# Attention and MoE in one kernel: the start written out by hand, with the first two batches alternating over d_ff

## The chip, the cores and the metric

The kernel runs on one core of a Trainium2 chip. The metric is the device time of one execution in microseconds (us), as the median of several runs. A profiled execution of the same program gives the trace that the following parts read.

## What is computed

The reference first runs a two-stage attention for 8 batches and 8 heads (sequence 576, head size 64, 32 packed queries `p`), and then a feed-forward layer on the 4608 x 512 result, with d_ff = 2048.

```python
def _attn_ref(q, k, v, p):
    scale = 1.0 / np.sqrt(q.shape[-1])
    def sm_attn(qq, kk, vv):
        s = scale * np.matmul(qq, kk.transpose(0, 1, 3, 2))
        s = s - np.max(s, axis=-1, keepdims=True)
        a = np.exp(s)
        a = a / (np.sum(a, axis=-1, keepdims=True) + 1e-09)
        return np.matmul(a, vv)
    p_packed = sm_attn(p, k, v)
    return sm_attn(q, p_packed, p_packed)

def _moe_ref(x, w_in, w_out):
    h = x @ w_in
    sp = np.where(h > 20.0, h, np.log1p(np.exp(np.minimum(h, 20.0))))
    return (h * np.tanh(sp)) @ w_out
```

The two weights arrive as float64 words, which the kernel converts itself.

## The kernel before

**The work of one batch.** Attention of a batch has two halves of four heads (`g`). Keys are turned on TensorE (PE) and copied out of PSUM (L118, L106), scores are taken, their largest value subtracted, and the exponential taken in one instruction for both halves (`score`, `exps`). Queries, the attention weights and the packed values follow (`turn`, `turn_weights`, `values`, `turn_values`); `match` takes the second scores and `weigh` their softmax, and leaves it as a high and a low part, `aT_hi` and `aT_lo`. The packed values never go into an output of attention: `packed_w` (L331) multiplies them into a chunk of four d_ff blocks of w_in (`ps_w`, L338), so that the first layer of the feed-forward part is one product of `wp_hi`, `wp_lo` with `aT_hi`, `aT_lo`.

**The main loop** (L501) has one step `t` for each block of 128 columns of d_ff of each batch: 16 steps a batch, 128 in all, and two more at the end. A step has the first product (`up`, two column halves, twelve matmuls, L388), Mish on ScalarE (ACT, L391 and L393), the split of the result `g` into `g_hi` (a cast) and `g_lo` on VectorE (DVE, L400 and L401, `halves`), and the second product (`down`, four row chunks of three matmuls, L405 to L407) of the block two steps earlier (`LAG`). Four accumulators of PSUM collect a batch's 16 blocks and are copied out after the last (`evac`). The last 64 columns of two batches are multiplied together, four blocks at a time (`split`, `down_rest`). Every fourth step ends with the `packed_w` of the next chunk. The attention of batch b+1 is a generator, of which up to three pieces are taken in each step of batch b; whatever is left is done before the batch's first `packed_w` (`together(gen)`).

**The weights.** There are 16 tiles of w_in (four chunks of four, `load_wi`) and 16 of w_out (`load_wo`). Each is loaded as pairs of 32-bit words into one of three staging buffers (`staged`, L304) and converted by two Copy instructions of ACT (L295, L296) and four operations of DVE (L297 to L302); w_out is then split into a high and a low part (L312, L313). Converted w_in goes to DRAM as well, from where later batches fetch it. Four tiles are converted during batch 0's attention, five ahead of the loop, and then two in each step, so all 32 are done by step 11.

**Order.** Only PE runs in the order in which the program is written (L474). The order of DVE, ACT and of the DMA queue (SP, from which every load and store is issued) comes from the planner, which fits each instruction in where its engine is free in a simulated run. Keys, queries and values share seven buffers of two heads each (`KVB`); a batch has twelve such tiles.

## Time and profile before

| | |
|---|---|
| median of three runs | 821.02 us (820.76 to 822.58) |
| the profiled execution's own time | 822.64 us |
| its span in the trace | 820.9 us |
| PE busy | 768.2 us (94%) |
| weight loads of PE | 610.4 us (74%) |
| DVE busy | 420.6 us (51%) |
| ACT busy | 336.0 us (41%) |
| moved by DMA | 90.02 MB, 110 GB/s over the span |

The span runs from the first instruction to the last. Times in the trace count from its start. A matmul's busy time is pipelined: the distance from one start to the next says how fast PE runs, and the granted clock (1 is full speed) whether it was throttled. In the strip of 40 slices a slice is 20.5 us and a digit is the busy share in tenths.

### The profile page before, as it was taken

The numbers are of one execution on the slowest core, as the hardware profiler recorded it, in microseconds if no ns is written. First come the engines' busy times: TensorE is split into PE (matmuls) and PEld (weight loads), VectorE is DVE, ScalarE is ACT, GpSimd is POOL, SyncE is SP. The second block draws the span as 40 slices with busy tenths as digits, with TensorE's granted clock in tenths as the row PEclk, the third lists the DMA queues.
The fourth block names the chain that finished last, engine by engine and source line by source line (L and its number), as shares of the span: only waits on it lengthen the run. The fifth ranks groups of instructions, "written<-read, shape, count | busy, mean of one in ns | idle before, by whom it ended". The sixth has DMA issues, their size and how long they took to land.

```text
span 820.9 us, 13745 instructions
## 1 busy us (share of the span) xinstructions
PE 768.2 (94%) x5584; PEld 610.4 (74%) x5584; DVE 420.6 (51%) x812; ACT 336.0 (41%) x766; POOL 0.7 (0%) x6
## 2 busy tenths in 40 slices
PE   6607789999999999999999999999999999999997
PEld 4406667787788787877778787877778787888886
DVE  4799895744373435544373435544373445533332
ACT  3557583435242353235242353335242353332221
POOL 0000000000000000000000000000000000000000
PEclk6557789999999999999999999999999999999999
DMA  9967673144311533144411433144311421131002
GB/s 256 287 226 231 207 243 95 52 139 138 110 52 52 143 95 111 52 138 139 110 52 52 132 107 111 52 137 140 110 52 52 122 67 53 52 103 52 1 1 64
DMA packets 43966, 90.02 MB, mean 110 GB/s; under 512 B 8576, under 2 KB 27008, under 8 KB 43904
## 3 DMA queue, kind: packets, MB, share of 16 engines
q1 hardware_dynamic: 43904, 89.15, 35.8%
q8 instruction: 44, 0.72, 0.4%
q14 instruction: 18, 0.15, 0.1%
HBM read 75.50 MB, written 13.63 MB: 109 GB/s over the span
## 4 chain that ended last, share of the span: by engine, by line
PE 88%; DMA 5%; DVE 4%; issue 1%; ACT 1%; SPq 0%; ACTq 0%
PE ps_h L388 25%; PE acc L405 16%; PE acc L407 14%; PE acc L406 14%; PE ps_kq L118 4%; DMA w_st<-in_moe_w_in_dram 4%; PE ps_w L338 4%; PE ps_s L127 3%; PE ps_rest L405 2%; PE ps_rest L407 2%; PE ps_rest L406 2%; PE ps_pp L209 1%; PE ps_a L200 1%; DMA k_t<-in_k_dram 1%; DMA w_st<-in_moe_w_out_dram 1%
## 5 line engine op out<-in xcount | busy, mean ns | idle before, releaser
L405 PE MATMUL acc<-wo_hi,g_hi 128*128 128x512 f32 x512 | 216.5, 423 | 0.0
L391 ACT ACTIVATE g<-ps_h 128x288 f32<-128x288 f32 (+1 forms) x256 | 98.5, 385 | 286.5 <-PE ps_h L388 250.5
L407 PE MATMUL acc<-wo_hi,g_lo 128*128 128x512 f32 x512 | 203.4, 397 | 0.0
L406 PE MATMUL acc<-wo_lo,g_hi 128*128 128x512 f32 x512 | 203.3, 397 | 0.0
L388 PE MATMUL ps_h<-aT_hi,wp_hi 128*128 128x288 f32 x512 | 159.3, 311 | 21.8 <-ACT aT_hi L263 21.1
L400 DVE CAST g_hi<-g 128x512 fp32r<-128x512 f32 x128 | 54.5, 426 | 239.7 <-ACT g L391 239.7
L388 PE MATMUL ps_h<-aT_lo,wp_hi 128*128 128x288 f32 x512 | 153.2, 299 | 1.9 <-DVE aT_lo L264 1.9
L388 PE MATMUL ps_h<-aT_hi,wp_lo 128*128 128x288 f32 x512 | 153.3, 299 | 0.0
L405 PEld LDWEIGHTS acc<-wo_hi,g_hi 128*128 128x128 f32 x512 | 97.4, 190 | 42.7 <-issue 20.4
L388 PEld LDWEIGHTS ps_h<-aT_hi,wp_hi 128*128 128x128 f32 x512 | 98.1, 192 | 39.6 <-ACT aT_hi L263 23.2
L407 PEld LDWEIGHTS acc<-wo_hi,g_lo 128*128 128x128 f32 x512 | 96.9, 189 | 23.7 <-DVE g_lo L401 0.2
L388 PEld LDWEIGHTS ps_h<-aT_lo,wp_hi 128*128 128x128 f32 x512 | 98.4, 192 | 11.3 <-DVE aT_lo L264 2.5
L406 PEld LDWEIGHTS acc<-wo_lo,g_hi 128*128 128x128 f32 x512 | 97.6, 191 | 8.6
L388 PEld LDWEIGHTS ps_h<-aT_hi,wp_lo 128*128 128x128 f32 x512 | 98.4, 192 | 0.0
L401 DVE TENSOR_TENSOR g_lo<-g,g_hi 128x512 fp32r<-128x512 f32 x128 | 88.2, 689 | 5.9
L350 DVE TENSOR_TENSOR wp_lo<-ps_w,wp_hi 128x512 fp32r<-128x512 f32 x64 | 41.3, 682 | 19.0 <-ACT wp_hi L349 19.0
L349 ACT CAST wp_hi<-ps_w 128x512 fp32r<-128x512 f32 x64 | 34.3, 588 | 32.8 <-PE ps_w L338 32.8
L338 PE MATMUL ps_w<-wi,ppT 64*32 64x512 f32 x512 | 35.7, 615 | 0.0
L118 PE MATMUL ps_kq<-ident,k_t 96*128 96x96 f32 x192 | 27.0, 273 | 9.0 <-issue 4.9
L118 PEld LDWEIGHTS ps_kq<-ident,k_t 96*128 96x128 f32 x192 | 23.1, 158 | 16.4 <-issue 6.4
L118 PE MATMUL ps_kq<-ident,q_t 96*128 96x96 f32 x192 | 26.6, 267 | 6.5 <-issue 2.9
L118 PEld LDWEIGHTS ps_kq<-ident,q_t 96*128 96x128 f32 x192 | 22.6, 154 | 13.1 <-issue 4.6
(81 smaller groups left out, 727.0 us busy)
## 6 DMA issues: line engine op xcount, KB each, us to landing
wi<-w_in_f SPq DMA_DIRECT2D x56, 512.0 KB, 4.5
k_t<-in_k_dram SPq DMA_DIRECT2D x32, 288.0 KB, 3.6
q_t<-in_q_dram SPq DMA_DIRECT2D x32, 288.0 KB, 4.8
v_t<-in_v_dram SPq DMA_DIRECT2D x32, 288.0 KB, 3.6
w_st<-in_moe_w_in_dram SPq DMA_DIRECT2D x16, 512.0 KB, 5.2
w_st<-in_moe_w_out_dram SPq DMA_DIRECT2D x16, 512.0 KB, 4.3
out_dram<-o SPq DMA_DIRECT2D x24, 192.0 KB, 2.5
w_in_f<-wi SPq DMA_DIRECT2D x8, 512.0 KB, 5.0
```

What stands on the lines that cost most here:

```text
L118: nc.tensor.transpose(out=ps[:, h, :], in_=of_slot(src, g, h)[:, i, :], identity=ident[:R, :R])
L127: nc.tensor.matmul(out=ps[u][h * NP:(h + 1) * NP, :], lhsT=packT[u * D:(u + 1) * D, h * NP:(h + 1) * NP], rhs=xT[u * D:(u + 1) * D, :, h, ...
L338: nc.tensor.matmul(out=ps[g][h * NP:(h + 1) * NP, :], lhsT=ppTb[row:row + D, g, h * NP:(h + 1) * NP], rhs=wis[b, c, g][row:row + D, h // 2 ...
L349: nc.scalar.copy(out=hi, in_=ps[g])
L350: nc.vector.tensor_tensor(out=lo, in0=ps[g], in1=hi.bitcast(F32), op=ALU.subtract)
L388: nc.tensor.matmul(out=ps, lhsT=w[:, fs], rhs=a[:, g, cs], start=(n == 0), stop=(n == 5))
L391: nc.scalar.activation(out=self.act[:, hf * HALF:hf * HALF + m], in_=ps[:, :m], func=AF.Mish)
L400: nc.vector.tensor_copy(out=hi, in_=self.act)
L401: nc.vector.tensor_tensor(out=lo, in0=self.act, in1=hi.bitcast(F32), op=ALU.subtract)
L405: nc.tensor.matmul(out=acc, lhsT=hi[:, cs], rhs=wh, start=start, stop=False)
L406: nc.tensor.matmul(out=acc, lhsT=hi[:, cs], rhs=wl, start=False, stop=False)
L407: nc.tensor.matmul(out=acc, lhsT=lo[:, cs], rhs=wh, start=False, stop=stop)
```

## The change

The change rewrites the start of the program. The parts are these:

- Ahead of the loop and in steps 0 to 9 (`START`), DVE, ACT and SP also run in the order in which the program is written. From step 10 on they are planned as before; PE is written throughout.
- The blocks run in another order: batch 0's blocks 0 to 7, batch 1's 0 to 15, batch 0's 8 to 15, then batches 2 to 7 as before (`TURNS`, `order`). Batch 0's accumulators are copied out as parts after its first turn, and added to the second turn's. A pair's rest product comes when the later of its two chunks is done (`paired`).
- A weight is an object with `fetch` (its load), `words` (the two Copies), `join` (the four operations of DVE) and `done` (the store, or the split of w_out). Of the first 16 weights, 14 are loaded into eight more buffers (tag `late`), which w_out's tiles 8 to 15 take over later; the others use two staging buffers. `conversion` fetches several weights ahead in the start and two ahead later. Two weights are converted in steps 0 and 1 and one in each later step.
- Batch 1's attention is taken in steps 0 to 5, up to five pieces a step. Batch 2's begins at step 20. Batches 2 and 3 are loaded at steps 12 and 24.
- Batch 0's attention takes the exponential straight from PSUM, the largest value as its bias, and gets the sum from the same instruction (`score_now`, `exps_now`).
- Copies out of PSUM in attention have a fixed engine (`ACT, DVE, ACT` for keys and queries; `ACT, DVE` for attention weights), in place of the planner's choice. In steps 0 to 9 the cast to `g_hi` is on ACT. `weigh` is cut in two (`peak`, `weigh`).
- `KVB` goes from 7 to 8, the buffers of `g` from 3 to 2. `wo_hi` and `wo_lo` are halves of one tile.

The diff, cut:

```diff
-KVB = 7
+KVB = 8
+EARLY = 16
+
+START = 10
+TURNS = [(0, 0, 8), (1, 0, 16), (0, 8, 16)]
...
-    def evacuate(dst, src, n=None):
-        if n is None:
-            nc.any.tensor_copy(out=dst, in_=src)
-        elif n % 2:
+    def evacuate(dst, src, by):
+        if by == "ACT":
             nc.scalar.copy(out=dst, in_=src)
         else:
             nc.vector.tensor_copy(out=dst, in_=src)
...
-            evacuate(dst[:, i, :, :], ps, i if pool is ps_acc else None)
+            evacuate(dst[:, i, :, :], ps, ("ACT", "DVE", "ACT")[i])
...
+        def turn_keys(self, g):
+            self.kT = att.tile([P, NI, 4, R], F32, name="kT", tag="T", bufs=2)
+            for _ in transposed(ps_acc, self.k_t[g], g, self.kT):
+                pass
+
+        def score_now(self, g):
+
+            self.s_ps = scores(ps_a, self.pT[:, g, :], self.kT)
+            mx = stat.tile([P, 2], F32, name="mx")
+            for u in range(2):
+                nc.vector.reduce_max(out=mx[:, u:u + 1], in_=self.s_ps[u], axis=AX.X)
+            self.top = stat.tile([P, 1], F32, name="top")
+            nc.vector.tensor_tensor(out=self.top, in0=mx[:, 0:1], in1=mx[:, 1:2], op=ALU.max)
+            nc.vector.tensor_scalar(out=self.top, in0=self.top, scalar1=-scale, scalar2=None, op0=ALU.mult)
+
+        def exps_now(self, g):
+            sm = stat.tile([P, 2], F32, name="sm")
+            for u in range(2):
+                nc.scalar.activation(
+                    out=self.a1[:, g, u].rearrange("a i r -> a (i r)"), in_=self.s_ps[u], func=AF.Exp,
+                    bias=self.top, scale=scale, accum_out=sm[:, u:u + 1],
+                )
+            return sm
+
+        def sums_now(self, g, sm):
+            rs = self.rs[:, g:g + 1]
+            nc.vector.tensor_tensor(out=rs, in0=sm[:, 0:1], in1=sm[:, 1:2], op=ALU.add)
+            nc.vector.tensor_scalar(out=rs, in0=rs, scalar1=1e-9, scalar2=None, op0=ALU.add)
+            nc.vector.reciprocal(out=rs, in_=rs)
...
-                evacuate(self.a1T[g][:, u], ps)
+                evacuate(self.a1T[g][:, u], ps, ("ACT", "DVE")[u])
...
+            if self.st is not None:
+                return
+            n = weights.index(self)
+            if n < EARLY and n % 10 < 8:
+                self.st = wts.tile([P, 2 * FC], I32, name="w_st", tag="late", bufs=NF // 2)
+            else:
+                self.st = wts.tile([P, 2 * FC], I32, name="w_st", tag="wstage", bufs=2)
+            nc.sync.dma_start(out=self.st, in_=self.source())
...
+        def words(self):
+            self.dst = self.place()
...
+            nc.scalar.activation(out=self.dst, in_=self.high.bitcast(F32), func=AF.Copy, scale=F64_SCALE)
+            nc.scalar.activation(out=self.r, in_=low.bitcast(U32), func=AF.Copy, scale=2.0 ** -29)
...
+        def done(self):
+            if self.i >= NF // 2:
+                wo.append(wts.tile([P, 2, DO], F32R, name=f"wo{self.i}", tag="late", bufs=NF // 2))
+            hi, lo = wo[self.i][:, 0], wo[self.i][:, 1]
+            nc.scalar.copy(out=hi, in_=self.dst)
+            nc.vector.tensor_tensor(out=lo, in0=self.dst, in1=hi.bitcast(F32), op=ALU.subtract)
...
-            self.act = moe.tile([P, MAIN], F32, name="g", tag="g", bufs=3)
+            self.act = moe.tile([P, MAIN], F32, name="g", tag="g", bufs=2)
...
+        def halves(self, cast):
             self.g = split_tiles()
             hi, lo = self.g
-            nc.vector.tensor_copy(out=hi, in_=self.act)
+            cast(out=hi, in_=self.act)
             nc.vector.tensor_tensor(out=lo, in0=self.act, in1=hi.bitcast(F32), op=ALU.subtract)
...
+    def evac(b, acc, c, last):
+
+        if not last:
+            o = parts[b, c] = wts.tile([P, DO], F32, name=f"part{b}{c}", bufs=1)
+        else:
+            o = wts.tile([P, DO], F32, name="o", tag="w2k", bufs=W2K)
+        if (b, c) in parts and last:
+            nc.vector.tensor_tensor(out=o, in0=acc, in1=parts[b, c], op=ALU.add)
+        elif c % 2 == 0:
             nc.scalar.copy(out=o, in_=acc)
         else:
             nc.vector.tensor_copy(out=o, in_=acc)
...
+    turns = TURNS + [(b, 0, NF) for b in range(2, B)]
+
+    order = [(b, f, f == a, f == e - 1) for b, a, e in turns for f in range(a, e)]
+    chunks = [(b, f // 4) for b, f, _, _ in order if f % 4 == 0]
+
+    paired = {}
+    for t, (b, f, _, _) in enumerate(order):
+        if f % 4 == 3:
+            paired[b // 2 * 2, f // 4] = t
+    paired = {t: x for x, t in paired.items()}
...
+    weights = [Weight(0, m) for m in range(4)] + [WeightOut(0)] + [Weight(1, m) for m in range(4)]
+    weights += [WeightOut(i) for i in range(1, 8)] + [Weight(2, m) for m in range(4)] + [WeightOut(8)]
+    weights += [Weight(3, m) for m in range(4)] + [WeightOut(i) for i in range(9, NF)]
+
+    def conversion(n):
+
+        while n < len(weights):
+            weights[n].join()
+            if n + 6 < EARLY:
+                weights[n + 6].fetch()
+            elif n + 2 < len(weights):
+                weights[n + 2].fetch()
+            yield
+            if n + 1 < len(weights):
+                weights[n + 1].fetch()
+                weights[n + 1].words()
+            weights[n].done()
+            n += 1
+            yield
...
+    def step(t, n_att, n_conv, cast):
+
+
+        nonlocal gen
+        grp = None
+        if t < len(order):
+            b, f, begin, end = order[t]
+            if t == 20:
+                gen = batches[2].attention()
+            if b > 1 and f == 0 and b + 1 < B:
+                gen = batches[b + 1].attention()
+            if b > 1 and f == 10 and b + 2 < B:
+                batches[b + 2].load()
+            grp = Group(b, f, begin, end, wps[b, f // 4], g_rests[b // 2])
+            grp.tiles()
+        groups.append(grp)
+        dn = groups[t - LAG] if t >= LAG else None
+        if dn:
+            down(dn, 0)
+        if grp:
+            grp.up(0)
+        take(conv, n_conv // 2)
+        take(gen, n_att[0])
+        if dn:
+            down(dn, 1)
+            down(dn, 2)
+        take(gen, n_att[1])
+        if grp:
+            grp.up(1)
+        take(conv, n_conv - n_conv // 2)
+        if grp:
+            grp.halves(cast)
+        if t - 1 in paired:
+            pb, i = paired[t - 1]
+            rest["g"] = split(g_rests[pb // 2][0, i], g_rests[pb // 2][1, i])
+        if dn:
+            down(dn, 3)
+        n = t // 4 + 1
+        if t % 4 == 2 and n < len(chunks):
+            nb, nch = chunks[n]
+            if nch == 0:
+                together(gen)
+            wps[nb, nch] = packed_w(nb, nch)
+            if n >= 7 and n + 1 < len(chunks):
+                fetch_wi(chunks[n + 1][1])
+        else:
+            take(gen, n_att[2])
+        if t - 2 in paired:
+            down_rest(*paired[t - 2])
+
...
+        first, second = batches[:2]
+        w = weights
+        with tc.manual_schedule(engines={mybir.EngineType.DVE, mybir.EngineType.Activation, mybir.EngineType.SP}):
+            first.load_k(0)
+            first.load_p()
+            first.load_k(1)
+            w[0].fetch()
+            first.load_q(0)
+            first.load_q(1)
+            w[1].fetch()
+            first.start(ps_a)
+            first.turn_keys(0)
+            first.score_now(0)
+            w[0].words()
+            sums = [first.exps_now(0)]
+            first.turn_keys(1)
+            first.load_v(0)
+            first.load_v(1)
+            w[2].fetch()
+            w[3].fetch()
+            w[0].join()
+            first.score_now(1)
+            w[1].words()
+            sums.append(first.exps_now(1))
+            together(first.turn(0, ps_acc))
+            w[1].join()
+            w[1].done()
+            w[4].fetch()
+            first.sums_now(0, sums[0])
+            together(first.turn_weights(0, ps_acc))
+            together(first.turn(1, ps_acc))
+            first.sums_now(1, sums[1])
+            second.load_k(0)
+            second.load_p()
+            second.load_k(1)
+            for n in (5, 6, 7, 8):
+                w[n].fetch()
+            w[2].words()
+            w[2].join()
+            for g in range(2):
+                together(first.values(g, ps_a))
+                if g == 0:
+                    together(first.turn_weights(1, ps_acc))
+            for g in range(2):
+                together(first.turn_values(g, ps_a))
+            w[3].words()
+            for g in range(2):
+                together(first.match(g, ps_acc))
+            for g in range(2):
+                second.load_q(g)
+            w[9].fetch()
+            for g in range(2):
+                first.peak(slice(g, g + 1))
+            w[3].join()
+            w[3].done()
+            first.weigh(slice(0, 1))
+            wps = {(0, 0): packed_w(0, 0)}
+            first.weigh(slice(1, 2))
+            w[4].words()
+            w[4].join()
+            w[10].fetch()
+            w[5].words()
+            w[4].done()
+            conv = conversion(5)
+            groups = []
+            gen = batches[1].attention()
+            g_rests = [{} for _ in range(B // 2)]
+            for t in range(START):
+                if t == 2:
+                    for g in range(2):
+                        second.load_v(g)
+                step(t, (1, 2, 2) if t < 6 else (1, 1, 1), 4 if t < 2 else 2, nc.scalar.copy)
+        for t in range(START, len(order) + LAG):
+            if t in (12, 24):
+                batches[t // 12 + 1].load()
+            step(t, (1, 1, 1), 2, nc.vector.tensor_copy)
```

More of the change, by code (lines that the diff above doesn't have):

```diff
@@ L78, in body @@
     ps_warm = ps_h.tile([P, P], F32, name="ps_warm", tag="ps_h")
-    wo_hi = [const.tile([P, DO], F32R, name=f"wo_hi{i}") for i in range(NF)]
-    wo_lo = [const.tile([P, DO], F32R, name=f"wo_lo{i}") for i in range(NF)]
+    wo = [const.tile([P, 2, DO], F32R, name=f"wo{i}") for i in range(NF // 2)]
     w_in_v = w_in.bitcast(I32).rearrange("(m p) f -> p m f", p=P)
@@ L277, in attention @@
                 yield from self.turn(g, ps_a)
+            self.sums()
             for g in range(2):
                 yield from self.turn_weights(g, ps_a)
-            for g in range(2):
                 yield from self.values(g, ps_a)
@@ new lines, in body, with __init__, source, place @@
+    class WeightOut(Weight):
+        def __init__(self, i):
+            self.i = i
+        def source(self):
+            return w_out_v[:, self.i, :]
+        def place(self):
+            return wts.tile([P, DO], F32, name="wo32", tag="w2k", bufs=W2K)
+        def done(self):
+            if self.i >= NF // 2:
[3 more added lines that the diff above has]
+            nc.vector.tensor_tensor(out=lo, in0=self.dst, in1=hi.bitcast(F32), op=ALU.subtract)
@@ L420, in down @@
         b, f, g = grp.b, grp.f, grp.g
-        if f == 0 and c == 0:
+        if grp.first and c == 0:
             accs[:] = [ps_acc.tile([P, DO], F32, name=f"acc{i}", tag="acc") for i in range(NCH)]
-        down_one(accs[c], g[0], g[1], slice(c * P, (c + 1) * P), f, f == 0, f == NF - 1)
+        down_one(accs[c], g[0], g[1], slice(c * P, (c + 1) * P), f, grp.first, grp.last)
+        if not grp.last:
+            return
+        o = evac(b, accs[c], c, f == NF - 1)
         if f < NF - 1:
             return
-        o = evac(accs[c], c)
         a = c * P
@@ new lines, in take @@
+    def take(it, n):
+        for _ in range(n):
+            next(it, None)
+    def step(t, n_att, n_conv, cast):
[45 more added lines that the diff above has]
+            down_rest(*paired[t - 2])
@@ L476, in body @@
             nc.tensor.matmul(out=ps_warm, lhsT=still, rhs=still, start=True, stop=True)
-        first = batches[0]
-        first.load()
-        convert(2)
-        first.start(ps_a)
-        together(first.score(0, ps_acc))
-        first.exps(slice(0, 1))
-        together(first.score(1, ps_acc))
-        first.exps(slice(1, 2))
-        together(first.turn(0, ps_a))
-        convert(2)
-        together(first.turn_weights(0, ps_acc))
-        together(first.turn(1, ps_a))
-        together(first.turn_weights(1, ps_acc))
```

192 lines of the change are left out of this document (70 added, 122 removed).

## The prediction

> **What bounds the kernel now.** I read the page's strip of busy tenths first, to see where TensorE (PE) is not full.
>
> ```profile
> span 820.9 us, 13745 instructions
> ...
> PE   6607789999999999999999999999999999999997
> ...
> DVE  4799895744373435544373435544373445533332
> ...
> PEclk6557789999999999999999999999999999999999
> DMA  9967673144311533144411433144311421131002
> ```
>
> From the seventh slice to the last but one (123 us to 800 us) PE is full at full clock. All that can be won lies in the first 123 us: there VectorE (DVE) has the high digits, PE has gaps, and the granted clock is low. The second view cuts the span at places that can be found again in the changed kernel.
>
> ```profile
> 8.30:53.40 45.10, 22.38 (x240) 14.56 (x240) 36.48 (x86) 23.37 (x43) 0.00 (x0) 0.54 0.96 279
> 53.40:117.90 64.50, 44.92 (x235) 35.75 (x235) 59.09 (x126) 44.46 (x87) 0.00 (x0) 0.72 0.70 218
> 117.90:258.70 140.80, 139.72 (x1091) 110.81 (x1097) 75.80 (x139) 59.03 (x136) 0.00 (x0) 1.00 0.31 95
> 258.70:444.38 185.68, 185.62 (x1400) 147.62 (x1407) 87.22 (x164) 73.56 (x173) 0.00 (x0) 1.00 0.33 99
> 701.39:738.93 37.54, 37.54 (x233) 30.90 (x240) 16.05 (x28) 11.45 (x32) 0.00 (x0) 1.00 0.27 85
> 738.93:782.06 43.13, 43.13 (x256) 35.37 (x263) 13.66 (x26) 11.33 (x33) 0.00 (x0) 1.00 0.07 25
> ```
>
> The columns are the stretch, its length, busy time of PE, weight loads, DVE, ScalarE (ACT) and GpSimd, the granted clock, the DMA share and GB/s. DVE is busy 59.09 of 64.50 us (92%) while PE is busy 44.92: there DVE sets the pace. After 117.90 PE is busy 139.72 of 140.80, DVE about half.
>
> The cuts are packed_w products, one in every fourth step of the main loop (a step is one d_ff block of one batch). The chain of waits and the timeline give them, and the matmuls of L388, twelve a step, count the steps.
>
> ```profile
> 117.90 1.09 PE L338 MATMUL ps_w<-wi,ppT 64*32 64x512 f32 x16
> ...
> 258.70 1.02 PE ps_w L338 x16
> ...
> 444.38 1.02 PE ps_w L338 x16
> ...
> 0.00:117.90 117.90, 20.21 (x84) 17.05 (x84) 0.67 0.81 241
> 117.90:258.70 140.80, 47.12 (x288) 42.47 (x288) 1.00 0.31 95
> ```
>
> So 84/12 = 7 steps lie before 117.90 (it closes step 6) and 24 between it and 258.70 (it closes step 30). By the end of step 30 both kernels have done the same work: 31 blocks, three batches' attention, three of the four rest products of the first pair, whatever the order of the blocks. From there on the code is alike and PE is full. **The change is worth the shift of this one event, 258.70.**
>
> **The change part by part.** First PE's price from the third of the steps on. A pair of batches takes 185.68. Eight steps without attention or rest take 37.54, eight with two rest products 43.13; so a rest product is (43.13 - 37.54)/2 = 2.8 us, and one attention (185.68 - 2 x 37.54 - 2 x 43.13)/2 = 12.2 us of PE. From step 6 to step 30 the new order has 24 steps (3 x 37.54 = 112.6), three rest products (8.4; they come in steps 13, 17 and 29) and the attention of batch 2 (12.2): 133.2 us if PE stays full. The old order took 140.8 because half of batch 1's attention was in it too. With P the start of the packed_w that closes step 6 and w the waits of steps 7 to 30, the event falls at P + 133.2 + w.
>
> P is a matter of DVE, so its work up to there is counted; from the groups of instructions before 117.90 (the answer has 39 DVE rows, the first and the last among those shown; their columns after the count are busy us and mean ns).
>
> ```profile
> L299 DVE SCALAR_TENSOR_TENSOR wi<-w_st,wi 128x512 int32<-128x512 int32 x16 | 10.8, 683 | 0.0
> L302 DVE CUSTOM_DVE_ANT_0 wi<-wi,wround 128x1024 uint16<-128x1024 uint16 x16 | 10.8, 679 | 0.0
> L299 DVE SCALAR_TENSOR_TENSOR wo<-w_st,wo 128x512 int32<-128x512 int32 x13 | 8.8, 680 | 0.0
> L313 DVE TENSOR_TENSOR wo_lo<-wo,wo_hi 128x512 fp32r<-128x512 f32 x12 | 8.2, 685 | 0.3 <-ACT wo_hi L312 0.3
> L302 DVE CUSTOM_DVE_ANT_0 wo<-wo,wround 128x1024 uint16<-128x1024 uint16 x12 | 8.1, 681 | 0.0
> L297 DVE TENSOR_SCALAR wi<-wi 128x512 f32<-128x512 f32 x16 | 6.8, 423 | 7.4 <-ACT wi L295 7.3
> L298 DVE TENSOR_SCALAR wi<-wi 128x512 int32<-128x512 int32 x16 | 6.6, 418 | 0.0
> L297 DVE TENSOR_SCALAR wo<-wo 128x512 f32<-128x512 f32 x14 | 5.8, 417 | 1.0 <-ACT wo L295 1.0
> L298 DVE TENSOR_SCALAR wo<-wo 128x512 int32<-128x512 int32 x13 | 5.4, 420 | 0.0
> ...
> L181 DVE TENSOR_SCALAR a<-ps_s,top 128x288 f32<-128x288 f32 x8 | 3.7, 508 | 0.0
> ...
> L400 DVE CAST g_hi<-g 128x512 fp32r<-128x512 f32 x7 | 3.0, 424 | 2.1 <-ACT g L391 2.1
> ...
> L112 DVE COPY kT<-ps_kq 128x384 f32<-128x384 f32 x4 | 2.2, 554 | 0.8 <-PE ps_kq L118 0.7
> ...
> L193 DVE RECIPROCAL rs<-rs 128x2 f32<-128x2 f32 x1 | 0.2, 161 | 0.0
> ```
>
> The 39 rows sum to 110.8 us; DVE was busy 95.7 (36.48 + 59.09 + 0.2 in the first 8.3), because neighbours overlap: 0.86 of the sum.
> - Weights. Before, 16 wi and 12 to 13 wo conversions are done by then, 71.3 us: 23 are written up to there, and the planner ran more ahead. Written out, the new order does 4 weights ahead of the loop (and begins the fifth), two a step in steps 0 and 1, then one: 8 wi at 2.20 and 6 wo at 2.88 by the end of step 6, 34.9 us. Saved: 36.4. This is the core: the alternating order needs w_out's second half only from step 16 on.
> - Casts. Steps 0 to 9 cast g_hi on ACT: seven of L400 go (3.0), a seventh L401 comes (0.7). Saved: 2.3. On ACT it lies beside DVE work.
> - Batch 0. The four subtractions of L181 go (2.0), and so does its sum of exponentials (accumulated by the Exp); more copies come (each 0.55). Saved: about 3.0, hidden under nothing, so counted.
> - Batch 1's attention, now finished in steps 0 to 5. DVE in one attention: (87.22 - 2 x 16.05 - 2 x 13.66)/2 = 13.9 us busy, with most copies on ACT; fixed ACT-DVE-ACT puts six of 0.55 more on DVE: 16.8. Before, 6.5 us of it lay ahead of 117.90 already. Added: 10.3.
>
> Busy to step 6: 95.7 - 0.86 x (36.4 + 2.3 + 3.0) + 10.3 = 70 us. Before, DVE was busy 81% of the stretch to 53.40 and 92% after. In the loop of the new order lie nine weights (0.86 x (4 x 2.20 + 5 x 2.88) = 20 us), one attention (16.8), the seven L401 and a pair of wp_lo (5): 42 us. The other 28 us, batch 0's attention and the first weights, are a chain of small dependent steps in written order: I take 75%, so the loop begins near 8.3 + 37 = 45. The 42 us I take at 85%, below the 92%, because no planner can now fill a wait: 49 us. **P = 94.** Bounds: 95% throughout gives 82, 65% gives 116.
>
> Waits the written order adds: on ACT a `words` (two Copy instructions) stands until its staging load has landed, with transposes' copies and Mish behind it and PE behind those; on SP a batch 1 load stands until a kv buffer is free, with weight loads 5 to 8 behind it. Eight more staging buffers and fetches several weights ahead cover both: the bytes up to the fourth weight are 12 x 288 + 2 x 64 + 4 x 512 KB = 5.8 MB, 21 us at the row's 279 GB/s, and DVE needs that weight after 30 us. Uncovered, ACT's wait of before would come back (20.5 us in the row below).
>
> For w I take 4 us, between 0 and 12: DVE has some 105 us (18 weights 40, three times 16.05 for 24 steps, one attention 16.8) in these 133 us of PE, fuller than the 75.80 of 140.80 before, and batch 2's attention overlaps the last conversions in steps 20 to 24. At nothing I cost the third turn's accumulator copies (batch boundaries of before hide the same ones under a full PE) and g's two buffers instead of three (PE asks for g_lo of a block before it starts the block that reuses its buffer).
>
> Sum: the event moves from 258.7 to 94 + 133.2 + 4 = 231, a gain of 27.5. The profiled execution took 822.64, 1.7 over its span; 822.6 - 27.5 = 795. The median run is 1.6 lower: **794**, that is, 696 + P + w.
>
> **PE's clock** is the weak place.
>
> ```profile
> 80.60 0.90 PE L118 MATMUL ps_kq<-ident,k_t 96*128 96x96 f32 x4 [3.47 <-DVE wp_lo L350]
> ...
> 81.78 0.63 PE L406 MATMUL acc<-wo_lo,g_hi 128*128 128x512 f32 x1
> 82.21 0.63 PE L407 MATMUL acc<-wo_hi,g_lo 128*128 128x512 f32 x1
> ...
> 121.72 0.55 PE L118 MATMUL ps_kq<-ident,q_t 96*128 96x96 f32 x4 [1.05 <-DVE wp_lo L350]
> ...
> 122.38 0.40 PE L406 MATMUL acc<-wo_lo,g_hi 128*128 128x512 f32 x1
> 122.61 0.39 PE L407 MATMUL acc<-wo_hi,g_lo 128*128 128x512 f32 x1
> ```
>
> After 3.47 us of idling the matmuls start 0.43 apart, after 1.05 us 0.23 apart: a long gap costs a factor of 1.87 on what follows. The Trainium skill ("TensorE: Matmul & The Clock Gate", Part 1) says that an idle window of about 3.4 us halves the clock and that as long a busy one restores it; these rows agree. By that rule, gaps of this length in every step of the start would leave PE cold to step 6, which is the second rival.
>
> **The rivals.**
> 1. DVE waits at the head of its written order (65% to 70% instead of 81%): P = 108 to 116, 808 to 816. For: ACT stands between most pairs of DVE steps. Against: weight joins are woven between them.
> 2. PE stays cold. Its warm work in steps 0 to 6 is 7 x 37.54/8 less two missing down products (2 x 12 x 0.23) plus 12.2 = 39.5 us; cold 74. Begun at 45, P = 119: 819, hardly a change. For: 0.72 clock in the loop's start before. Against: there are only 39.5 us of work in 49 us, so a gap of 3.5 us in each step doesn't fit.
> 3. Slower: the staging of weights 16 to 31. They have two buffers, not three.
>
> ```profile
> L295 ACT ACTIVATE wi<-w_st 128x512 f32<-128x512 f32 x16 | 10.8, 674 | 20.6 <-DMA w_st<-in_moe_w_in_dram 20.5
> ...
> w_st<-in_moe_w_in_dram SPq DMA_DIRECT2D x16, 512.0 KB, 5.2
> ...
> 32.94 12.04 DMA w_st<-in_moe_w_in_dram
> ```
>
> A buffer is held for the landing, two Copies (1.35) and three DVE operations (1.5): with 5.2 to land, 8.1/2 = 4.0 us a weight, under the 5.5 of a step (133.2/24). With 12.04, as once in the chain, 7.4 us: 16 x 1.9 = 30 us lost and 824. It turns slower once landing averages 11.5 us. For: batch 2's loads enter the queue at step 12. Against: the queue moved 95 GB/s there, a third of what it can.
> 4. Better: written order without gaps, 95%, w = 0: 778.
>
> **How the numbers follow.** Forecast (P 84 to 105, 782 to 808) 0.68; rival 1 0.13; rival 2, or an order that does not bring the start forward at all, 0.06; rival 3 0.06; rival 4 0.07. The range of 8 in 10 is 781 to 811: the forecast, part of 1 and of 4. Within 0.2% of the median (1.6 us, about what can be told from no change) falls half of rival 2: 0.03. Faster 0.90, slower 0.07.
>
> **What would show it.** Right: the third packed_w near 94 and the ninth near 231; the granted clock near 0.9 in steps 2 to 6; full PE from then on; 14 weights converted by then, not 28. Wrong: an ACT Copy waiting on a staging load with PE idle over 3 us (rivals 1, 2), or gaps in PE after step 9 released by a weight's conversion (rival 3). A gain in the start that is given back by step 30 would break the claim that the shift of one event is the whole effect.

## The result, and the profile after

The changed kernel is slower: 834.73 us median of 4 runs (832.19 to 836.21) against 821.8 us of 4 runs before, a ratio of 1.0153 with an interval of [1.0122, 1.0184]. The profiled execution took 832.19 us. The forecast was 794, with 811 as the upper end of its range.

These are the strips of the changed kernel's page, those that were shown of before. A slice is 20.8 us here.

```profile
span 830.4 us, 13713 instructions
...
PE   8557748899999999999999999999999999999997
...
DVE  5776565788446653735373444636373454633332
...
PEclk9658977999999999999999999999999999999999
DMA  9946200552352444115311443125411421122002
```

PE is not full until the ninth slice (before: the seventh), and DVE, which showed 9, 9, 8, 9 in slices three to six, now shows 7, 6, 5, 6. Neither engine is full. The same shows in a view of busy time by stretch, cut at the loop's start as forecast and at the two events of the forecast, the packed_w products that close step 6 and step 30 (columns: stretch, length, PE, weight loads, DVE, ACT, GpSimd, granted clock, DMA share, GB/s).

```profile
8.30:45.00 36.70, 22.11 (x232) 12.70 (x230) 28.17 (x63) 15.16 (x33) 0.00 (x0) 0.76 1.07 320
45.00:118.10 73.10, 50.93 (x380) 38.43 (x381) 47.02 (x88) 36.34 (x69) 0.00 (x0) 0.77 0.35 109
118.10:270.47 152.37, 140.36 (x934) 110.03 (x933) 101.78 (x196) 73.39 (x167) 0.00 (x0) 0.97 0.34 108
```

Batch 0's stage came out as counted: 28.17 us of DVE in 36.70, 77%. The loop's first product starts at 39.2, waits 3.47 us for a cast of `aT_hi` and goes on at 44.2, so the loop begins near 45. The loop itself did not come out as counted. Its stretch up to P took 73.10 us instead of 49, with DVE busy 47.02, 64%. From P to the event (the start of the packed_w that closes step 30) it took 152.37 instead of 137. The cuts are these rows of the timeline (start, duration).

```profile
75.41 1.09 PE L430 MATMUL ps_w<-wi,ppT 64*32 64x512 f32 x16
...
118.10 1.09 PE L430 MATMUL ps_w<-wi,ppT 64*32 64x512 f32 x16
...
151.82 1.09 PE L430 MATMUL ps_w<-wi,ppT 64*32 64x512 f32 x16
...
270.47 1.09 PE L430 MATMUL ps_w<-wi,ppT 64*32 64x512 f32 x16
```

These rows close steps 2, 6, 10 and 30. So P is 118.1 (forecast 94) and w is 270.5 - 118.1 - 133.2 = 19.2 (forecast 4). Steps 7 to 10 take 33.7 us; four steps of full PE are 37.54/2 = 18.8, so 15 of the 19 are lost there.

Who kept PE waiting from 44 to 150 us? These are PE's waits: operation, releaser, sum, number, longest.

```profile
PE acc L498 <- ACT wo L413: 15.2, 6, 6.3
PE ps_kq L122 <- ACT kT L114: 4.8, 2, 4.3
PE ps_h L481 <- ACT aT_hi L320: 3.5, 1, 3.5
PE ps_kq L122 <- issue: 3.3, 1, 3.3
PE ps_pp L262 <- DVE a1T L116: 3.1, 2, 2.7
```

The largest wait is for the cast of a w_out tile to its high part (L413, in `done`), which ACT does. DVE's own waits from 45 to 118 say the same: 14.1 of the 26.1 us in which DVE was idle there ended with this cast, which its subtraction (L414) needs.

```profile
DVE wo L414 <- ACT wo L413: 14.1, 5, 4.6
```

The timeline shows how one such wait of PE comes about (at the head of step 6; idle time and its releaser in brackets).

```profile
106.66 1.16 ACT L305 ACTIVATE a<-a 128x1152 f32<-128x1152 f32 x1 [4.84 <-DVE a L302]
107.84 1.28 ACT L484 ACT_TABLE_LOAD   x1
109.14 0.36 ACT L484 ACTIVATE g<-ps_h 128x224 f32<-128x224 f32 x1
...
109.50 0.66 ACT L380 ACTIVATE wo<-w_st 128x512 f32<-128x512 f32 x1
110.05 0.66 ACT L381 ACTIVATE wround<-w_st 128x512 int32<-128x512 uint32 x1
110.59 0.62 ACT L413 CAST wo<-wo 128x512 fp32r<-128x512 f32 x1
...
111.27 0.79 PE L498 MATMUL acc<-wo,g_hi 128*128 128x512 f32 x1 [6.31 <-ACT wo L413]
```

Read it upwards. PE's `down` needs the wo cast. In ACT's written order that cast stands behind the two Copies of the *next* weight, these behind Mish of step 5's second half, and Mish behind the Exp of batch 1's attention, which itself waits 4.84 us for DVE. None of these needs the one ahead of it; they only stand in one line. The next wait, 4.21 us at 123.40, has two casts of the same attention (`aT_hi`, L320) at the head of the line.

Why is the tile asked for so late? The list of weights has `wo[k]` at place 8 + k (k from 1 to 7). Step t multiplies with `wo[t-2]`, place t + 6. The loop converts two weights in steps 0 and 1 and one in each later step, so it finishes place t + 6 in the second half of step t - 1, right ahead of the `down` that needs it. So each of the steps 3 to 9 has a ring, a chain of waits that leads from one step into the next: `up`, Mish, Copies, cast, `down`, `up`.

### The profile page after: what moved, and what is told of

Read it like the earlier page. It is cut to its first block, busy times and chain, and to the rows that moved or that the text cites. A ratio compares the mean times of both kernels' runs of the same rounds, so it can differ in the third digit from the quotient of the medians.

```text
span 830.4 us, 13713 instructions
## 1 busy us (share of the span) xinstructions
PE 774.9 (93%) x5584; PEld 613.4 (74%) x5584; DVE 444.7 (54%) x846; ACT 321.8 (39%) x740; POOL 0.7 (0%) x6
## 4 chain that ended last, share of the span: by engine, by line
PE 83%; DVE 6%; DMA 5%; ACT 4%; issue 1%; SPq 0%; DVEq 0%; ACTq 0%
PE ps_h L481 24%; PE acc L498 14%; PE acc L499 13%; PE acc L500 13%; PE ps_kq L122 4%; PE ps_w L430 3%; PE ps_s L131 3%; DMA w_st<-in_moe_w_in_dram 3%; PE ps_rest L498 2%; PE ps_rest L500 2%; PE ps_rest L499 2%; PE ps_pp L262 2%; DMA w_st<-in_moe_w_out_dram 1%; PE ps_a L253 1%; ACT wround L381 1%
## 5 line engine op out<-in xcount | busy, mean ns | idle before, releaser
L498 PE MATMUL acc<-wo,g_hi 128*128 128x512 f32 x512 | 216.0, 422 | 16.8 <-ACT wo L413 15.2
L499 PE MATMUL acc<-wo,g_hi 128*128 128x512 f32 x512 | 204.2, 399 | 0.9 <-DVE wo L414 0.9
L500 PE MATMUL acc<-wo,g_lo 128*128 128x512 f32 x512 | 203.5, 397 | 0.1
L493 DVE CAST g_hi<-g 128x512 fp32r<-128x512 f32 x118 | 50.2, 426 | 198.5 <-ACT g L484 198.5
L481 PE MATMUL ps_h<-aT_hi,wp_lo 128*128 128x288 f32 x512 | 154.1, 301 | 0.1
L498 PEld LDWEIGHTS acc<-wo,g_hi 128*128 128x128 f32 x512 | 97.5, 191 | 60.2 <-issue 22.8
L500 PEld LDWEIGHTS acc<-wo,g_lo 128*128 128x128 f32 x512 | 97.4, 190 | 22.8 <-DVE g_lo L494 0.5
L499 PEld LDWEIGHTS acc<-wo,g_hi 128*128 128x128 f32 x512 | 97.7, 191 | 11.1 <-DVE wo L414 3.0
L441 ACT CAST wp_hi<-ps_w 128x512 fp32r<-128x512 f32 x64 | 34.4, 591 | 28.1 <-PE ps_w L430 28.1
L430 PE MATMUL ps_w<-wi,ppT 64*32 64x512 f32 x512 | 37.6, 615 | 4.5 <-DVE wi L392 4.5
```

The lines of the kernel that those rows point to most:

```text
L430: nc.tensor.matmul(out=ps[g][h * NP:(h + 1) * NP, :], lhsT=ppTb[row:row + D, g, h * NP:(h + 1) * NP], rhs=wis[c, g][row:row + D, h // 2, : ...
L441: nc.scalar.copy(out=hi, in_=ps[g])
L481: nc.tensor.matmul(out=ps, lhsT=w[:, fs], rhs=a[:, g, cs], start=(n == 0), stop=(n == 5))
L493: cast(out=hi, in_=self.act)
L498: nc.tensor.matmul(out=acc, lhsT=hi[:, cs], rhs=wh, start=start, stop=False)
L499: nc.tensor.matmul(out=acc, lhsT=hi[:, cs], rhs=wl, start=False, stop=False)
```

## The experiments

Three theories stood at first. **A**: the late w_out tile and its place behind the Copies. **B**: batch 1's attention, packed into the written order of eight steps. **C**: the staging of weights with two buffers. D to G came from the results. The table has all runs; the cuts are the starts of the packed_w that close steps 2, 6, 10 and 30, from each run's timeline. A cut comes from one execution, the median from several. The last matmuls of the packed_w written ahead of the loop start between 34.4 and 38.4 us, although all runs but e3, e4 and e7 have the same code up to there. So a difference of two cuts is good to some 4 us.

| kernel | median us | ratio to before, interval | step 2 | step 6 | step 10 | step 30 |
|---|---|---|---|---|---|---|
| before | 821.8 | 1 | 74.4 | 117.9 | 143.1 | 258.6 |
| the change | 834.73 | 1.0153 [1.0122, 1.0184] | 75.4 | 118.1 | 151.8 | 270.5 |
| e1_one_ahead | 821.05 | 0.9995 [0.9975, 1.0016] | 78.9 | 114.8 | 142.7 | 258.9 |
| e2_hi_first | 825.28 | 1.0037 [1.0018, 1.0055] | 78.6 | 118.2 | 146.9 | 265.1 |
| e3_planned_loop | 822.57 | 1.0003 [0.9989, 1.0017] | 87.4 | 113.3 | 144.5 | 261.3 |
| e4_three_stage | 831.78 | 1.0116 [1.0081, 1.0151] | 79.0 | 121.8 | 154.1 | 271.4 |
| e5_tail_pieces | 818.09 | 0.9956 [0.9933, 0.9979] | 77.1 | 110.7 | 137.6 | 254.0 |
| e6_no_attention | 781.86 | 0.9513 [0.9488, 0.9539] | 58.6 | 82.3 | 101.1 | 218.7 |
| e7_sequential | 823.87 | 1.0028 [1.0004, 1.0052] | 68.6 | 113.6 | 144.2 | 261.0 |
| e8_attention_first | 810.50 | 0.9856 [0.9839, 0.9874] | 74.7 | 104.1 | 129.6 | 247.7 |
| e9_both_first | 812.77 | 0.9887 [0.9871, 0.9902] | 74.0 | 104.9 | 132.6 | 249.8 |
| e10_tail_hi | 818.72 | 0.9958 [0.9945, 0.9970] | 75.9 | 110.8 | 138.5 | 256.4 |
| e11_order_alone | 826.05 | 1.0048 [1.0030, 1.0066] | 74.1 | 120.7 | 146.5 | 264.3 |
| e12_order_one_ahead | 813.63 | 0.9903 [0.9884, 0.9923] | 75.4 | 110.7 | 135.3 | 253.1 |
| e13_kept_warm | 811.32 | 0.9877 [0.9858, 0.9895] | 72.3 | 103.2 | 128.8 | 247.4 |

**The late w_out tile.** e1 converts two weights in step 2 as well, so that every later tile is done a step earlier.

```diff
-                step(t, (1, 2, 2) if t < 6 else (1, 1, 1), 4 if t < 2 else 2, nc.scalar.copy)
+                step(t, (1, 2, 2) if t < 6 else (1, 1, 1), 4 if t < 3 else 2, nc.scalar.copy)
```

> Edit: two weights are converted in step 2 as well (as in steps 0 and 1), so that from step 3 on every weight is one step earlier than in the changed kernel. Theory A (late weight: in steps 3 to 9 PE stands at the head of the step for the w_out tile whose last cast sits on ACT behind the step's own Mish and two Copies): the 17 us of PE waiting for ACT wo_hi between 75 and 190 us go nearly whole, and part of the half-clock matmuls after them; the third packed_w (118.1 us) comes 6 to 10 us earlier and the time falls by 15 to 20 us, to 815 to 820. Theory B (the short chains of batch 1's attention in a fixed order set steps 0 to 6, the weight is incidental): the third packed_w moves by less than 3 us, the time by less than 4. Theory C (two staging buffers for weights 16 to 31): no gain, 832 to 838.

It took 13.7 us off the change, and in PE's waits of the same window no row for L413 is left. The largest is now this one:

```profile
PE ps_h L481 <- ACT g L484: 5.2, 1, 5.2
```

What stands ahead is again the tail of batch 1's attention, here its two casts of `aT_hi` with Mish behind them, now seen by the next product:

```profile
119.94 0.67 ACT L320 CAST aT_hi<-at 128x576 fp32r<-128x576 f32 x1 [4.94 <-DVE at L319]
122.24 0.67 ACT L320 CAST aT_hi<-at 128x576 fp32r<-128x576 f32 x1 [1.64 <-DVE at L319]
122.82 0.65 ACT L484 ACTIVATE g<-ps_h 128x288 f32<-128x288 f32 x2
...
123.28 0.61 PE L481 MATMUL ps_h<-aT_hi,wp_hi 128*128 128x288 f32 x1 [5.15 <-ACT g L484]
```

The median is 821.05, 1 us above theory A's 815 to 820, and the packed_w of step 6 came 3.3 us earlier, not 6 to 10, while theory B had it move by less than 3. A is right about the wait, which is a third of the miss (13.7 of 40.7 us); a part of the time waited only passed to what stood next in line.

e2 leaves the weights' timing and only writes a tile's own cast ahead of the next one's Copies.

```diff
+            weights[n].done()
             if n + 1 < len(weights):
                 weights[n + 1].fetch()
                 weights[n + 1].words()
-            weights[n].done()
```

> Edit: inside conversion the cast of the finished weight is written ahead of the two Copies of the next one, so on ACT it stands 1.2 us earlier in each step; nothing else moves. Theory A: each of steps 3 to 9 gets about 1.2 us shorter where PE stands for that cast, 6 to 9 us in all, 825 to 829. Theories B and C: within 2 us of 834.7.

It gained 9.5 us, with three quarters of the wait left:

```profile
PE acc L498 <- ACT wo L413: 11.4, 5, 5.3
```

825.28 us lies at the edge of theory A's 825 to 829. The waits named shrink by 3.8 us and the median by 9.5. The waits come from the profiled executions, though, and these two differ by 5.1 us (832.19 and 827.05), so most of the gap is scatter between executions. The lateness of the tile itself is still there.

**Staging.** e4 gives the late weights three buffers, and takes one from keys, queries and values to make room.

```diff
-KVB = 8
+KVB = 7
...
-                self.st = wts.tile([P, 2 * FC], I32, name="w_st", tag="wstage", bufs=2)
+                self.st = wts.tile([P, 2 * FC], I32, name="w_st", tag="wstage", bufs=3)
```

> Edit: three staging buffers of the ordinary kind instead of two (and 7 buffers for keys, queries and values, as before, to make room). Theory C: weights 16 to 31 come earlier, the seven staging loads on the chain between 142 and 184 us shrink, 8 to 15 us gained. Theories A and B: the third packed_w stays at 118 and steps 11 to 30 give at most 4 us, 830 to 835.

The median is 3 us lower, as theories A and B had it (830 to 835), not C's 8 to 15. The event of step 30 stands at 271.4, but in this execution the packed_w ahead of the loop was already 3.1 us later (38.39 against 35.27); counted from there the event is 2.2 us earlier. C falls as the main cause. Since the run changed KVB too, what a third buffer brings by itself stays open.

**Written order or planner.** e3 plans DVE, ACT and SP in steps 0 to 9 again and keeps the written order ahead of the loop (the loop moves out of the inner `manual_schedule`, with nothing else changed).

```diff
-            for t in range(START):
+        for t in range(START):
```

> Edit: only the part ahead of the loop stays in written order on DVE, ACT and SP; steps 0 to 9 are left to the planner (their casts stay on ACT). Theory A: the planner can bring weights forward, the waits for wo_hi go, 812 to 820. Theory B: the chains of batch 1's attention are filled too, third packed_w at 95 to 105, 805 to 815. Theory C: the waits of steps 11 to 30 (about 4 us) stay, the third packed_w does not move, 831 to 836. If written order is better than the planner's, the time goes up above 837.

12 us better than the change, the planner's version ends where before did, and lies in none of the ranges expected. It loses at the start and wins later: its packed_w of step 2 is 12 us later than in the change, and steps 3 to 6 take 25.9 us instead of 42.7.

```profile
87.40:113.30 25.90, 25.10 (x265) 19.39 (x265) 11.86 (x21) 10.62 (x23) 0.00 (x0) 1.00 0.30 87
```

PE is full there at clock 1. DVE is busy only 11.86 us, since the planner had run the weights ahead: 16 of them were converted before step 2 closed. So steps with batch 1's attention can run at PE's pace when the weights are out of the way; the price here is the late end of step 2.

e7 also goes back to the old order of blocks: batch 0 whole, then batch 1, the loop planned, two weights a step, attention from step 2, the casts to `g_hi` on DVE.

```diff
-TURNS = [(0, 0, 8), (1, 0, 16), (0, 8, 16)]
+TURNS = [(0, 0, 16), (1, 0, 16)]
```

> Edit: written order only ahead of the loop; in the loop the planner, casts on DVE, and the old order of blocks (batch 0's 16 blocks, then batch 1's), two weights a step, batch 1's attention from step 2 on, three pieces a step. Beside the planned loop with alternating batches (822.6) it tells what alternating brings. If alternating brings the start forward (my reason in the prediction): 830 to 840, as DVE has all 32 weights in the first 14 steps again. If alternating costs what it saves, because batch 1's attention is due by step 8 and not by step 16: 812 to 822, since the loop begins 10 us earlier than in the kernel before.

823.87, between the two expectations and next to e3. With the planner in the loop the alternation over d_ff, together with the casts on ACT, is worth 1.3 us, less than these runs tell apart.

**Batch 1's attention.** e6 stands on e1 and leaves it out.

```diff
-            gen = batches[1].attention()
+            gen = iter(())
+            second.ppT, second.aT_hi, second.aT_lo = first.ppT, first.aT_hi, first.aT_lo
```

> Left out, on top of the run with one more weight in step 2 (821.0): the whole attention of batch 1; batch 1 uses batch 0's packed values and attention, everything else stays. It prices that attention in steps 0 to 6. If it costs only PE's own 12.2 us: 807 to 811. If its chains set the pace of steps 0 to 8 (theories B1 and B2): the third packed_w at 75 to 88 instead of 114.8, steps 7 to 10 at full PE, 775 to 792. If the weights' rate sets the pace (a theory D: DVE and ACT cannot make one weight a step): the third packed_w stays above 100 and the time above 800.

All three signs of theory B are there: the packed_w of step 6 at 82.3 (75 to 88 expected), steps 7 to 10 in 18.75 us, which is full PE, and 781.86 us (775 to 792). The "theory D" of this expectation, a limit by the weights' rate, falls with it. The event of step 30 moved 40.2 us, of which PE's own work for an attention is 12.2. Without it DVE is as busy up to P as I had assumed with it, and from there to step 30 little is lost: 136.40 us against 133.2.

```profile
45.00:82.30 37.30, 31.67 (x157) 25.54 (x156) 31.56 (x57) 26.78 (x60) 0.00 (x0) 0.84 0.78 231
82.30:218.70 136.40, 133.26 (x933) 106.98 (x932) 96.95 (x188) 70.20 (x160) 0.00 (x0) 1.00 0.39 120
```

31.56 of 37.30 is 85%. And 218.7 + 12.2 = 230.9 is the forecast's event, 231. The second match is in part chance: without the attention's 16.8 us the forecast's sum of DVE work was 42 - 16.8 = 25, not 31.56 (11 weights are converted in this stretch, the forecast had nine). What it does show is that the forecast priced the attention as work to be laid beside the rest, its waits as if they were within the 85%.

e5, on e1, cuts the tail of this attention (`peak` and `weigh`) into five pieces, so that its Exp and its casts stand behind a Mish and not ahead of it.

```diff
-            self.peak(slice(0, 2))
             yield
-            self.weigh(slice(0, 2))
+            nc.scalar.activation(out=a2, in_=a2, func=AF.Exp, scale=scale)
+            yield
...
+                nc.vector.transpose(out=at, in_=self.a2[:, g].rearrange("a g n -> a (g n)"))
+                yield
+                nc.scalar.copy(out=self.aT_hi[:, g, :], in_=at)
```

> Edit, on top of the run with one more weight in step 2 (821.0): the tail of batch 1's attention (largest value, Exp, sums, casts) is cut into five pieces, so that on ACT the Exp and the two aT_hi casts stand behind Mish instead of ahead of it. Theory B1 (what is left is the tail standing at the head of ACT's written order: ACT waits 6.7, 4.9 and 1.6 us for DVE, and PE 1.8 and 5.2 us for Mish): those two PE waits go, with the half-clock stretch after them, 6 to 10 us, 811 to 815. Theory B2 (the whole attention of batch 1 is too much for eight steps, wherever its tail stands): the wait moves to the first block of batch 1 in step 8, less than 3 us gained.

3.0 us by the medians, 4.9 by the event: right in sign, about half of theory B1's 6 to 10, and at the edge of B2's "less than 3"; the intervals of e1 and e5 just touch. The two waits of PE named there (1.8 and 5.2 us) gave way to one of 4.82 us in step 7, which stands behind the same two casts. The chain of waits shows what was left in the loop (start, duration, what; in this kernel L508 is `up`, L511 Mish, L407 and L408 the Copies).

```profile
50.53 0.41 ACT g L511
50.95 0.57 ACT wi L407
51.52 0.55 ACT wround L408
52.07 0.38 ACT kT L114
52.49 0.90 PE ps_kq L122 x4
53.39 1.51 PE ps_h L508 x6
54.92 0.36 ACT g L511
55.39 0.55 ACT wi L407
55.94 0.55 ACT wround L408
```

It is a second ring of the same kind. A piece of attention on PE needs a PSUM buffer that ACT's copy of kT frees, and this copy stands behind Mish and two Copies. Its wait is the row `ps_kq <- ACT kT` of above, 4.3 us in one piece.

e8, on e5, writes a piece of attention ahead of the weight's work in each half of steps 0 to 9.

```diff
-        take(conv, n_conv // 2)
         take(gen, n_att[0])
+        take(conv, n_conv // 2)
...
+        if t < START and t % 4 != 2:
+            take(gen, n_att[2])
         take(conv, n_conv - n_conv // 2)
```

> On e5_tail_pieces, in steps 0 to 9 a piece of batch 1's attention is written ahead of the weight's work of the same half of the step, so that ACT's copies of kT, qT and a1T stand ahead of the two Copies and of the wo cast, and no longer behind them. Theory D (what is left of the loss is the ring PE, ACT, PE of the attention: a piece's matmuls wait for a copy on ACT that stands in the written order behind the Copies, 1.1 us each half-step, in the 8 steps that hold attention): PE's waits for kT and qT at L122 and L131 (some 8 us in e5_tail_pieces) fall to under 3, the packed_w of step 6 starts at 104 to 108 instead of 110.7, and the median falls by 3 to 7 us, to 811 to 815. Theory E (the weights' words decide; putting them later costs as much as the attention gains): the packed_w of step 6 stays within 2 us of 110.7 and the median within 3 us of 818, or rises, with PE waiting for wo at the down product again.

810.50 us, P 104.1: theory D holds for P and for the gain, half a microsecond better than its range. PE's waits for kT and qT fell from 8.1 to 3.9 us, not to under 3. This version beats before by 1.4% and the change by 2.9%. Steps 3 to 6 of e8 at full clock:

```profile
74.70:104.10 29.40, 25.42 (x266) 19.58 (x266) 22.61 (x43) 14.55 (x33) 0.00 (x0) 1.00 0.52 147
```

e9 and e10 add e2's order to e8 and e5.

> As e8_attention_first, and a w_out tile's own hi cast and lo subtract are written ahead of the next weight's fetch and two Copies, as in e2_hi_first. If e8_attention_first turns out to wait for wo, this takes 2 to 4 us of that wait away; if the late w_out tile was already settled by the one weight taken earlier (theory A as e1_one_ahead left it), the median is within 2 us of e8_attention_first.

> As e5_tail_pieces, with the w_out tile's hi cast and lo subtract ahead of the next weight's fetch and two Copies, as in e2_hi_first, and the attention where it was. Theory A says that the late tile costs nothing once it is taken one step earlier, since no wait for it is left in e5_tail_pieces: within 2 us of 818. If the order of conversion itself matters beyond that, 2 to 5 us faster.

Neither gains: 812.77, which is 2.3 us more than e8, and 818.72. Once the tile is a step early, its cast may stand behind the Copies.

e11 and e12 take e8's order without the others: e11 alone on the change, e12 with e1 but without the pieces of the tail.

> The changed kernel with nothing but the new place of the attention's pieces ahead of the weights' work in steps 0 to 9 (no weight taken earlier, the tail of the attention whole). If the two rings add (the attention's behind the Copies, worth some 7 us; the late w_out tile, worth 14), this takes 5 to 9 us off the changed kernel: 826 to 830, still with some 10 to 15 us of PE waiting for wo. If the late tile is the ring that decides and the attention hides under it, under 3 us: 832 to 836. If the tile is late only because the attention holds PE up, the wait for wo goes as well: under 822.

> Order and one weight earlier, without the five pieces of the attention's tail: the tail's share once the two rings are gone. If the three add, 3 us above e8_attention_first: 812 to 815. If the tail matters more now that nothing else holds the loop, 816 to 819. If it matters no more, within 1.5 us of 810.5.

The parts add. The order is worth 8.7 us alone (834.73 to 826.05) and 7.6 on top of the others (818.09 to 810.50), the late tile 13.7 alone and 12.4 on top of the order (826.05 to 813.63), the tail 3.0 on e1 and 3.1 on top of the other two. In e11 PE's wait for the w_out tile grows beyond the 10 to 15 us expected:

```profile
PE acc L498 <- ACT wo L413: 18.0, 6, 12.8
```

The new order puts the whole tail ahead of step 5's weight work: the Exp, which waits 5.58 us for DVE, and both casts of `aT_hi`, which wait 2.47 and 1.64 us, now stand ahead of one w_out cast. In the change they were split over two waits, of 6.31 and 4.21 us.

**PE's clock.** What is left between e8 and the forecast is 247.7 - 230.9 = 16.8 us, and 16.1 of the 29.0 us between e8 and e6 lie in steps 0 to 2 (74.7 against 58.6; PE's own work for the attention is among them), at a granted clock of 0.61. e13 is meant to keep PE warm there, that is at full clock, with 34 matmuls of zeros.

```diff
+    def fill(n):
+        ps = ps_acc.tile([P, P], F32, name="ps_fill", tag="acc")
+        for _ in range(n):
+            nc.tensor.matmul(out=ps, lhsT=still, rhs=still, start=True, stop=True)
```

> e8_attention_first with 34 idle matmuls of 128x128 zeros on PE in the gaps of steps 0 and 1 (4 behind the first packed_w, 7 between the halves of the first up product, 8, 10 and 5 beside the attention's pieces; one such matmul takes some 0.47 us cold and half of it warm), so that PE doesn't drop to half clock. It leaves nothing out. In e8_attention_first the clock granted from 47 to 74.7 us is 0.61 and PE is busy 19.6 of 27.7 us. Theory F (what is left of the loss in steps 0 to 2 is half clock: PE's pieces of the attention and of the up products stand in the chain at twice their length): the clock from 47 to the packed_w of step 2 rises above 0.9, that packed_w moves from 74.7 to 67 to 71, and the median falls by 3 to 8 us, to 803 to 807. Theory G (the chains through DVE and ACT set the pace, and PE has time to be slow): the clock rises but the packed_w of step 2 stays within 2 us of 74.7, and the median within 2 us of 810.5. If the idle matmuls stand in the way of the real ones, up to 4 us slower.

First e8, then e13, in the view by stretch:

```profile
47.00:74.70 27.70, 19.60 (x118) 15.28 (x118) 20.70 (x44) 18.71 (x35) 0.00 (x0) 0.61 0.40 123
```

```profile
47.00:60.00 13.00, 10.44 (x63) 8.51 (x63) 10.33 (x23) 9.52 (x20) 0.00 (x0) 0.63 0.19 62
60.00:74.70 14.70, 12.02 (x101) 9.26 (x100) 10.85 (x22) 9.29 (x17) 0.00 (x0) 0.98 0.67 199
```

From 60 us on the clock is 0.98; in e8 it was 0.65 from 60 to 74.7. The packed_w of step 2 comes 2.4 us earlier, but 2.3 of that are there ahead of the first added matmul (the second part of the packed_w before the loop starts at 34.36 against 36.64). The event of step 30 is 0.3 us earlier, counted from that packed_w 2.0 us later, and the median is 811.32. From 47 to 60 us the added matmuls did not hold the clock, so F is refuted only for the second half of these steps. There G holds: PE has time to be slow, and the packed_w of step 2, with PE at full clock, waits 0.97 us for ACT's copy of qT. That the added matmuls themselves took back some gain is not excluded.

## Why the prediction was wrong

**The step that failed** is "The 42 us I take at 85%, below the 92%, because no planner can now fill a wait: 49 us." The 42 was near: 47.02 measured, which at 85% would have made 55 us. The 85% was 64%, and that made it 73. The rate was borrowed from stretches in which DVE has a queue of ready weights. In the written order the chains of waits between the engines set the length, and busy time says nothing of them. The right question was, for one step, what each instruction at the head of ACT's and DVE's lines waits for, and what stands behind it. It could have been asked before any run: the place of `wo[t-2]` in the list follows from the code, and so does the order of `words` and `done`.

**"For w I take 4 us, between 0 and 12"** failed with it: 19.2, of which 15 in steps 7 to 10, for the same reason. I bounded it by DVE's sum and by batch 2's attention, and neither was late.

Where the 39.5 us of the missed event (270.5 against 231) went, by the cuts: 11.5 to the late tile (e1), 4.9 to the tail of batch 1's attention at the head of ACT's line (e5), 6.3 to the attention's copies behind the Copies (e8), and 16.8 that go with batch 1's attention (e6), whose place in the chains between PE, DVE and ACT no run takes apart further. By the medians the same four are 13.7, 3.0, 7.6 and 16.4 of 40.7 us. So the causes of 24 us are shown by runs, and of the other 16 only that they vanish when the attention is left out.

Point by point:
- **The event carries the whole effect**: right. The median is 562.1 to 564.3 us above the event in the change, e1, e5, e6 and e8 (before: 821.8 - 258.6 = 563.2), and 560.2 to 563.9 in the other runs, while the event itself moves by 52 us.
- **The loop begins near 45**: right, and batch 0's stage is at 77%, where I took 75%.
- **Weights**: right. 8 w_in and 5 w_out conversions are done by P, 13 where I counted 14. The saving shows: DVE was busy 28.17 + 47.02 from 8.3 to P, against 95.57 before in as many us. It was not the bound any more, so what was saved came out as idle time.
- **"On ACT it lies beside DVE work"**: wrong as a cover. ACT was the engine with the line. Moving work to it costs what stands behind.
- **Rival 1** (DVE waits at the head of its written order) had the right picture for P: 108 to 116 at 65% to 70%, against 118.1 at 68% (75.19 of 109.8 us from 8.3 on). But it had a chance of 0.13, and it kept w at 4. DVE waited at its head for ACT, and ACT at its own head for DVE.
- **Rival 2** (PE cold): the clock was 0.77 in the loop up to P, not the 0.9 that the forecast named as its sign. The long gaps cause it. Two waits in PE's timeline show the difference:

```profile
123.40 0.79 PE L498 MATMUL acc<-wo,g_hi 128*128 128x512 f32 x1 [4.21 <-ACT wo L413]
...
128.29 0.63 PE L499 MATMUL acc<-wo,g_hi 128*128 128x512 f32 x1
128.72 0.63 PE L500 MATMUL acc<-wo,g_lo 128*128 128x512 f32 x1
...
132.45 0.50 PE L498 MATMUL acc<-wo,g_hi 128*128 128x512 f32 x1 [1.46 <-ACT wo L413]
...
134.77 0.39 PE L499 MATMUL acc<-wo,g_hi 128*128 128x512 f32 x1
135.00 0.39 PE L500 MATMUL acc<-wo,g_lo 128*128 128x512 f32 x1
```

  After 4.21 us of idling the products are 0.43 us apart until 129, after 1.46 us they are 0.23 apart. The Trainium skill ("TensorE: Matmul & The Clock Gate", Part 1) puts the drop behind an idle window of about 3.4 us; these two waits agree. The prediction's rows showed only the drop of the clock; its return took 6 us of full PE after the wait at 123.40 and 4.5 us after the one at 111.27. The low clock is mainly a consequence here: without the waits for the tile, e1's steps 3 to 10 take 63.8 us instead of 76.4, and in e13 a higher clock alone brought nothing.
- **Rival 3** (the slower one, staging): slower was right and the mechanism wrong. All loads of w_in landed in 7.8 us (median); of those for weights 16 to 31, two issued near 70 us took 9.0, and from 130 us on six of w_in took 3.9 and eight of w_out 3.7, all below the 11.5 from which it decides.

```profile
w_st<-in_moe_w_in_dram SPq DMA_DIRECT2D x16, 512.0 KB, 7.8
```

- **At nothing** I put the accumulators' copies at the new turns. PE waited for such a copy once, 1.55 us at 150.93.
- **What would show it wrong**: ACT Copies did wait for staging loads, 20.1 us in all from 118 us to the event and 3.5 at most, but PE was not idle with them: from 140 us on it waited 4.3 us, in no case with a weight as the releaser. The forecast had no rival with a w_out tile that is late by order and not by load.

The Trainium skill ("Perfetto Trace Analysis", Tensor Engine Instruction) says that ACT, DVE and GpSimd are strict first-in, first-out. The rows from 106.66 to 111.27 agree: a Mish whose product had ended by 104.3 stood behind an Exp that waited 4.84 us, and started at 109.14.

## What to carry to other kernels

Before an order is written by hand, draw one step as a ring: for each wait, what stands behind it on that engine and who asks for that, and give every tile at least one step between its last operation and its first use. A sum of busy time bounds a stretch from below only; it is a forecast only where an engine has ready work queued. Where two streams share one engine, write the one on which PE waits first: here that was worth 8 us and cost no instruction.

## What was not expected of the hardware

Each change between Exp and Mish on ACT costs a table load, 1.28 us in the row at 107.84, and the Mish behind it starts at 109.14, as soon as the load ends. Both kernels have 30 such loads, and the forecast left them out. In a written order they stand in the line like any other instruction.

After the wait at 123.40 the slow clock lasted 6 us of full PE (until 129.4), so one wait of 4.21 us cost two thirds as much again behind it: nine products of `down` at 0.43 instead of 0.23 and eight of `up` at 0.24 instead of 0.13 make 2.7 us.

The staging loads of w_in landed slower than before by the median of all (7.8 against 5.2 us), but the slow ones are those of the start: the eight issued up to 60 us, most of them while the queue moved 320 GB/s (8.3 to 45 us), took 8.4, the two near 70 us 9.0 and the six from 130 us on 3.9. Why the two took so long is open.
